# Attention and FFN on one core: another transfer rate in the planner, a mask that arrives as bf16, and the global tokens' keys in two halves

## The chip, the cores and the metric

The kernel runs on one core of a Trainium2 chip. Its time is the device time of one execution in microseconds (us). Before the change the median of three runs is 917.84 us (917.44 to 918.08). Engines are named as in the profile: PE (TensorE) multiplies matrices, DVE (VectorE), ACT (ScalarE) and POOL (GpSimd) work on vectors, SP issues the transfers (DMA). SBUF is the core's memory; PSUM is where PE leaves its results.

## The reference, cut to what matters

There are 8 batches of 8 heads, 512 local and 32 global tokens per head, and a head size of 64. A local token attends to the 32 global tokens and to the local tokens at most 32 positions away; a global token attends to all 544. The 8 x 544 rows of 512 features that result go through an FFN with 2048 hidden features. All is float32.

```python
k_all = np.concatenate([k_g, k_l], axis=2)
s_g = scale * np.matmul(q_g, k_all.transpose(0, 1, 3, 2))
out_g = np.matmul(sm(s_g), v_all)
mask = np.abs(pos[:, None] - pos[None, :]) <= 32
s_ll = np.where(mask, scale * q_l @ k_l.T, -1e9)
out_l = np.matmul(sm(concat([scale * q_l @ k_g.T, s_ll])), v_all)
...
h = x @ w_in
g = h * erf(log(1 + exp(h)))
return g @ w_out
```

## The kernel before, in words

**Attention.** The host lays the keys of a head out as 24 blocks of 32: the global block stands several times among the 16 local ones, so that any window of four neighbouring blocks is one run of 128 columns. Two heads make a pair, 32 pairs in all; a pair's queries and keys (`qk`), and its values in two parts (`va`, `vb`), come in three transfers. For a pair PE makes 2 x 16 small products, 64 rows by 32 columns of the array each (`scores`, L466). A head's 512 x 128 scores stand in one PSUM bank. Heads 0 to 27 are "early" (`PREMASK = 27`, tested on the first head of a pair): PE first multiplies the identity with a bf16 mask into the bank (two more matmuls a pair), DVE then only takes the row maximum (`TENSOR_REDUCE mx<-s`), and ACT does the exponentials. In later heads DVE adds the float32 mask and finds the maximum in one custom operation, four per head (`mask_max`, L493), and DVE or POOL subtracts. The bf16 mask and identity (`mask16`) are made by DVE at the start from the float32 constants `cs` (`shorten`, L395). Probabilities are turned for the product with the values: for the first `TURN = 26` heads by PE transposes (four a head, `tr(S..., SM..., ident)`), for the others by DVE in blocks and a trip of transfers through memory (`blocks`, `move`).

**Global tokens.** Every four heads make a tile of global tokens, 16 tiles in all (`attention_global`, L676). `whole_keys` (L685) gives each head a column group of 32 of the array: four products with 480 columns into the bank `ga`, then four with 64 into `gb`. DVE takes two maxima and combines them, ACT does two exponentials into `pg`. The first `GTURN = 7` tiles are turned by six PE transposes, the others by DVE and transfers. Then come 24 products with the values and a normalisation.

**FFN.** Weights and activations are split into a high and a low float32r part, so each product is three matmuls. Weights come in 512 KB pieces that DVE, ACT and POOL convert (`top_in`, `winh`, `winl`). FFN work of batch 0 begins while attention of the later batches runs; a second pass over the other half of the hidden features follows.

**The order.** Every piece of work is added to a `Program` with a cost per engine that may do it, a key (its priority), and the buffers it reads and writes. `schedule` (L142) plays the program with these costs on a clock of its own and writes down the order in which the engines take the work; the kernel that runs has that order fixed, and an instruction waits only for its data. A transfer costs in the plan `DMA_START`, its KB divided by `DMA_RATE` on one shared bus, `DMA_END` and `NOISE`; a piece of PE work whose inputs come from another engine or from SP counts as ready `SLACK["PE"]` later. Of the first `FEW` transfers at most `DEPTH = 5` are in flight, and the kernel enforces that with a dependency. Until `FILL` on the planner's clock, PE gets idle matmuls (`spare`) wherever the plan has nothing for it; a filler is planned at 0.11, and at 0.22 up to `COLD = 3.5`:

```python
def cools():
    return now < COLD or now < FILL and sum(h for t, h in warmth[-200:] if t > now - TICK) < HEAT
...
if e == "PE" and until[e] <= now and cools():
    fill()
```

How many fillers stand between two pieces of PE work is thus decided when the kernel is built; on the chip they run in order whether or not the data is already there. The names that follow (`HKEYS`, `QLEAD`, `VLEAD`, `STEP`, `GOFF`, `WOUT`, `SUMS` and so on) are keys and offsets of keys. `FIRST` is the number of heads that borrow FFN buffers. `GA`/`GB`, `S` and the products' banks come from six PSUM banks.

Of the kernel before, what the change touches and what calls it, by code (L numbers as in the profile page):

```python
# [30 lines left out]
QLEAD, VLEAD, RLEAD, XLEAD = (1.003, -0.044), (0.254, 0.012), -0.513, (1.017, 1.142, 1.769)  # L31
GOFF, POFF = (1.794, 2.207, 2.003), (3.921, 2.901, 4.335)
WIN, WOUT = (-1.712, -2.919, 0.936, -1.237), (9.919, 7.526, 7.174, 2.651)
LATE = (52.485, 55.408, 57.308, 59.719, 62.13, 62.366, 66.952, 69.363)
BIAS, AHEAD = 0.801, 10.994

HARM = 0.759
SLACK, PORT = {"PE": 0.827, "SP": 0.663}, 0.65
# [14 lines left out]
SWITCH, TRADE, CHOICE = 0.068, 0.092, 1  # L53

NBIAS, PREMASK = 20, 27

SPAN = 7
ORDER = ((0, 1, 2, 3, 4, 5, 6, 8, 7), (7, 0, 1, 2, 3, 4, 5, 6, 8))
SEVEN = (0, 1, 2, 3, 4, 5, 6)
SUMS = (82.024, 82.124)  # L60

TURN, GTURN = 26, 7
# [32 lines left out]
class Program:  # L95
# [3 lines left out]
    DMA_START, DMA_END, DMA_RATE = 1.62, 1.0, 300.0  # L99
# [203 lines left out]
def kernel(  # L303
# [69 lines left out]
    def fixed(t):  # L373
        b = Buf(None, None, None, None, None)
        b.ap = t
        return b

    def load(key, dst, src, kbytes, deps=(), also=()):
        add({"SP": 0.45}, key, lambda: dma(dst.ap, src), reads=deps, writes=[dst, *also], moved=kbytes)

    cs = attn.tile([P, 512 + P + 64 + 2], F32, name="cs")
    CS = fixed(cs)
    mask = cs[:, :512].rearrange("p (t k) -> p t k", k=P)
    ident = cs[:, 512 : 512 + P]
    sel = cs[:, 512 + P : 512 + P + 64]
    half = cs[:, 512 + P + 64 :]
    load(HKEYS[0][1] - QLEAD[0] + 0.001, CS, cst, 360)
    PG = fixed(attn.tile([P, NENT // 4, P], F32, name="pg"))
    M16 = Buf(mp, [P, 512], F32, "mask16", "os", 2)

# [46 lines left out]
    def attention(b, h, key):  # L437
# [76 lines left out]
        if early:  # L514
            add({"DVE": 0.6}, key, lambda: dve.tensor_reduce(MX.ap, S.ap, axis=AX.X, op=ALU.max), [S], [MX])
            add({"ACT": 1.4}, key, scaled_exps, [S, TAB], [SM, MX])
        else:
            add({"DVE": 0.85}, key, mask_max, [S, CS], [SM, MX])
# [30 lines left out]
        if h % 2 == 1:  # L549
            PT = wide([P, 4, 2 * P], f"pt_{nm}", "pt")  # L550
            move(TP, PT, 2 * P, nm, key + STEP * 2)
            for i, n in enumerate((st["kept"], nm)):
                O = psum_a([P, 4, P], f"o_{n}")
                lhs = lambda t, a, i=i: PT.ap[:, a, P * i + WB * t : P * i + WB * t + WB]
                weighted(b, h - 1 + i, n, key, O, PT, lhs, (VA, VB, XN))

    def weighted(b, h, nm, key, O, PT, lhs, tiles):
# [15 lines left out]
        add({"PE": 0.64}, key + STEP * 3, values, [PT, VA, VB], [O], heat=1040, fetch=64, mode=1)  # L573
# [102 lines left out]
    def attention_global(b, j, key):  # L676
        nm = f"{b}_{j}"
        VA = [st["va", i] for i in range(2)]
        qks = [st["qk", i] for i in range(2)]
        GA, GB = (psum_a([P, 512], f"{x}_{nm}") for x in ("ga", "gb"))  # L680
        lane, block = lambda m, hh: hh, lambda m, hh: m
        whole_keys(key, nm, qks, GA, GB)
        global_values(b, j, nm, key, GA, GB, VA, lane, block)

# [39 lines left out]
    def global_values(b, j, nm, key, GA, GB, VA, lane, block):  # L724
# [42 lines left out]
        RS = abuf([P, 1], f"gr_{nm}", "gr", 2)  # L767

        def norm():
            dve.tensor_scalar(RS.ap, O.ap[:, D : D + 1], 1e-9, None, op0=ALU.add)  # L770
            dve.reciprocal(RS.ap, RS.ap)
            dve.tensor_scalar(HALF.ap, half, RS.ap, None, op0=ALU.mult)
# [14 lines left out]
        add({"DVE": 0.5}, key + STEP * 3, norm, [O, CS], [RS, HALF])  # L787
# [72 lines left out]
    def fetch_x(ps, c, key):  # L860
# [15 lines left out]
        if 0 < c < B:  # L876
            add({"SP": 1.8}, key, by_blocks, deps, [RX], moved=1260, issues=4)
        else:
            add({"SP": 0.45}, key, whole, deps, [RX], moved=2.048 * n)
# [365 lines left out]
    for ps in range(2):  # L1245
        for c in ORDER[ps]:
# [6 lines left out]
            if ps == 1 and c in SEVEN:  # L1253
# [35 lines left out]
def _layout(q_l, k_l, v_l, q_g, k_g, v_g, moe_w_in, moe_w_out):  # L1289
# [13 lines left out]
    vw = ones(vw.transpose(0, 1, 3, 2, 4))  # L1303
    qk = np.concatenate([qT, kE], axis=3)
# [5 lines left out]
    wo = np.ascontiguousarray(moe_w_out).view(np.int64).reshape(2, 4, 2, P, 512)  # L1310
    cst = np.zeros((P, 512 + P + 64 + 2), np.float32)
# [40 lines left out]
```

## Time and profile before

| | |
|---|---|
| median of three runs | 917.84 us |
| the profiled execution | 917.4 us, of which the span of its instructions 915.6 us |
| PE, DVE, ACT, POOL busy | 98%, 69%, 58%, 35% of the span |
| mean granted PE clock | 0.998 |
| transfers | 150.49 MB, mean 164 GB/s |

Busy time is the union of an engine's instructions; PE's matmuls overlap (the next starts while one drains), so a busy PE need not be at its peak. Idle time is put down to what ended it: an engine, a transfer, or "issue" where the profile shows nothing that the engine waited for. The granted clock is 1.0 at 2.4 GHz and 0.5 at 1.2 GHz. The rows that matter stand below.

### The profile page before, as it was taken

To read this page: it belongs to the slowest core of one execution; us is meant where nothing else is said; L and a number is where in the kernel's file an instruction comes from. 1 tells how busy PE (TensorE), PEld (TensorE's weight loads), DVE (VectorE), ACT (ScalarE), POOL (GpSimd) and SP (SyncE) were. 2 spreads that over 40 slices of the span, in tenths; PEclk is the share of its full clock that TensorE was granted. 3 is DMA by queue.
4 is the path that set the end of the run, shared out by engine and by line. 5 is a ranking of instruction groups with operands and counts; after the bars stand their busy time and mean duration, and the time that the engine had idled before them with its cause. 6 is when DMAs were issued, how large, how long until landed. Compare 5 with 4: busy or idle time off the path is not lost.

```text
span 915.6 us, 23027 instructions
## 1 busy us (share of the span) xinstructions
PE 899.7 (98%) x9367; PEld 747.7 (82%) x9367; DVE 635.5 (69%) x1473; ACT 527.2 (58%) x965; POOL 322.7 (35%) x251
## 2 busy tenths in 40 slices
PE   9889999999999999999999999999999999999998
PEld 7667777776777787778888888889999999999996
DVE  2699998755556666665589897956767676767543
ACT  3476987626654566275676665557555454545561
POOL 0021446422435253251147447444343433331300
PEclk9999999999999999999999999999999999999999
DMA  8688969677987778795451510312224140402113
GB/s 330 242 310 291 327 218 306 208 232 192 340 231 239 234 225 293 223 284 188 151 161 65 190 47 0 69 47 48 66 73 102 38 138 1 138 23 94 47 46 115
DMA packets 90761, 150.49 MB, mean 164 GB/s; under 512 B 11680, under 2 KB 53664, under 8 KB 90656
## 3 DMA queue, kind: packets, MB, share of 16 engines
q1 hardware_dynamic: 90464, 148.77, 51.2%
q8 instruction: 73, 1.20, 0.5%
q10 hardware_dynamic: 192, 0.26, 0.1%
q14 instruction: 32, 0.26, 0.1%
HBM read 109.81 MB, written 39.19 MB: 163 GB/s over the span
## 4 chain that ended last, share of the span: by engine, by line
PE 79%; DVE 11%; ACT 3%; POOL 3%; issue 3%; DVEq 0%; ACTq 0%; POOLq 0%
PE op L341 34%; PE h L341 32%; PE s L341 5%; DVE top_in L362 3%; DVE top_out L362 3%; PE spare L341 2%; PE o L341 2%; PE ga L341 2%; PE go L341 1%; POOL sp L362 1%; PE s L342 1%; DVE sx L362 1%; ACT sm L343 1%; ACT gh L343 1%; POOL sx L362 1%
## 5 line engine op out<-in xcount | busy, mean ns | idle before, releaser
L341 PE MATMUL op<-wouth,gh 128*128 128x512 f32 x544 | 216.8, 398 | 0.8 <-DVE rs L362 0.6
L341 PE MATMUL op<-woutl,gh 128*128 128x512 f32 x544 | 212.4, 390 | 0.0
L341 PE MATMUL op<-wouth,gl 128*128 128x512 f32 x544 | 212.1, 390 | 0.0
L362 POOL TENSOR_TENSOR sp<-sp,hs 128x512 f32<-128x512 f32 x77 | 110.5, 1456 | 213.3 <-ACT sp L343 202.4
L341 PE MATMUL h<-xh,winh 128*128 128x512 f32 (+1 forms) x464 | 165.2, 356 | 0.0
L341 PE MATMUL h<-xh,winl 128*128 128x512 f32 (+1 forms) x464 | 162.2, 350 | 0.0
L341 PE MATMUL h<-xl,winh 128*128 128x512 f32 (+1 forms) x464 | 162.1, 349 | 0.0
L362 DVE TENSOR_TENSOR hs<-h,hs 128x256 f32<-128x256 f32 x196 | 77.3, 420 | 65.0 <-PE h L341 51.8
L341 PEld LDWEIGHTS op<-wouth,gh 128*128 128x128 f32 x544 | 102.2, 188 | 24.4 <-issue 2.0
L341 PEld LDWEIGHTS op<-wouth,gl 128*128 128x128 f32 x544 | 102.1, 188 | 22.0
L341 PEld LDWEIGHTS op<-woutl,gh 128*128 128x128 f32 x544 | 102.3, 188 | 18.5
L344 ACT ACT_TABLE_LOAD x90 | 115.5, 1283 | 2.3 <-PEq L1339 0.7
L343 ACT ACTIVATE hs<-h 128x512 f32<-128x512 f32 (+1 forms) x76 | 41.8, 553 | 119.2 <-PE h L341 118.2
L362 POOL TENSOR_TENSOR gl<-sp,gh 128x512 fp32r<-128x512 f32 x58 | 82.5, 1427 | 73.7 <-ACT gh L343 54.9
L341 PEld LDWEIGHTS h<-xh,winh 128*128 128x128 f32 x464 | 87.8, 189 | 13.3 <-issue 0.8
L343 ACT ACTIVATE gh<-sp 128x512 fp32r<-128x512 f32 x111 | 67.5, 628 | 53.8 <-PE op L341 26.4
L341 PEld LDWEIGHTS h<-xh,winl 128*128 128x128 f32 x464 | 87.8, 189 | 11.7
L343 ACT ACTIVATE sp<-hs 128x512 f32<-128x512 f32 x136 | 76.9, 623 | 35.3 <-DVE hs L362 34.9
L341 PEld LDWEIGHTS h<-xl,winh 128*128 128x128 f32 x464 | 87.9, 189 | 11.0
L362 DVE TENSOR_TENSOR gl<-sp,gh 128x512 fp32r<-128x512 f32 x78 | 74.5, 973 | 11.4 <-ACT gh L343 9.2
L343 ACT ACTIVATE sp<-sp 128x512 f32<-128x512 f32 x136 | 74.9, 620 | 0.4
L362 DVE TENSOR_TENSOR sp<-sp,hs 128x512 f32<-128x512 f32 x59 | 62.5, 1071 | 9.9 <-ACT sp L343 9.3
(181 smaller groups left out, 1525.6 us busy)
## 6 DMA issues: line engine op xcount, KB each, us to landing
vb<-in_vB_dram SPq DMA_DIRECT2D x32, 650.0 KB, 6.0
qk<-in_qk_dram SPq DMA_DIRECT2D x30, 656.0 KB, 7.0
rx<-xsc SPq DMA_DIRECT2D x52, 256.0 KB, 5.2
va<-in_vA_dram SPq DMA_DIRECT2D x32, 390.0 KB, 5.9
px<-tp SPq DMA_DIRECT2D x76, 128.0 KB, 5.3
pt<-px SPq DMA_DIRECT2D x19, 512.0 KB, 5.3
raw_in<-in_w_in_dram SPq DMA_DIRECT2D x16, 512.0 KB, 4.4
xsc<-xT SPq DMA_DIRECT2D x32, 256.0 KB, 5.0
```

The source lines that it names most:

```text
L341: pe = lambda n, *a, **k: pinned(nc.tensor.matmul(n, *a, **k))
L342: tr = lambda *a, **k: pinned(nc.tensor.transpose(*a, **k))
L343: act = lambda *a, **k: pinned(nc.scalar.activation(*a, **k))
L344: table = lambda name: pinned(nc.scalar.preload_act_table_set(name))
L362: return lambda *a, **k: pinned(f(*a, **k))
```

## The change

- The planner's transfer: `DMA_RATE` 300 to 400 KB/us, start 1.62 to 1.5, end 1.0 to 0.9, `NOISE` 1.096 to 0.4. The cost of an activation fetch in blocks is given as 1700 KB in place of 1260.
- The constants come in three transfers in place of one. The first 160 KB are the mask and the identity as bf16, made by the host, into `mask16`; then identity, selector and halves as float32 (100 KB planned) into `ci`; later, by the key `MLEAD`, the float32 mask (262 KB planned) into `cs`. In the plan's keys the first stands just ahead of the first `qk`, the second just behind it. `shorten` on DVE is gone.
- From global tile 6 on (`GSPLIT = 6`, ten of 16 tiles) `half_keys` replaces `whole_keys`: eight products of 384 columns, one for each of the four column groups and two row groups of the array: the keys are cut into two halves that stand in different column groups, the even and odd head of a pair go to `ga` and `gb`. DVE takes two maxima, exchanges them between the halves in four small operations and combines them in a fifth; ACT does four exponentials. The global block that is then met twice has its values zeroed by the host (`vw[..., NWIN - 1] = 0.0`).
- `PREMASK` 27 to 26 (13 pairs with the mask from PE, where there were 14), `TURN` 26 to 24, `GTURN` 7 to 8, `FIRST` 12 to 16, `FEW` 68 to 70, `FILL` 52.16 to 53.627.
- The normalisation of a global tile keeps its sum in PSUM and multiplies with a tensor operation in place of a scalar one.
- `NBIAS` 20 to 19, and keys, offsets and weights of the planner are set anew (`HKEYS`, `STEP`, `GKEY`, `VLEAD`, `XLEAD`, `GOFF`, `WIN`, `WOUT`, `LATE`, `SUMS`, `HARM`, `SLACK["SP"]`, `SWITCH`, `TRADE`). `MERGE` and `PLAIN` are new and off.

```diff
-SINCE, COLD, FILL, TICK, HEAT = 0.75, 3.5, 52.16, 3.41, 3200
-HKEYS = ((0, -7.978), (4, -4.315), (22, 1.593), (28, 6.473), (64, 43.98))
-STEP, GKEY = 0.008, (-0.119, -0.115, -0.139)
+SINCE, COLD, FILL, TICK, HEAT = 0.75, 3.5, 53.627, 3.41, 3200
+HKEYS = ((0, -7.978), (4, -4.315), (22, 1.593), (26, 7.644), (64, 44.103))
+STEP, GKEY = 0.023, (-0.152, -0.148, -0.172)
...
-FIRST = 12
+FIRST = 16
-DEPTH, FEW = 5, 68
-LANES, NOISE = 8, 1.096
+DEPTH, FEW = 5, 70
+LANES, NOISE = 8, 0.4
-NBIAS, PREMASK = 20, 27
+NBIAS, PREMASK = 19, 26
+MLEAD = -5.966
-SUMS = (82.024, 82.124)
-TURN, GTURN = 26, 7
+SUMS = (81.085, 83.737)
+TURN, GTURN = 24, 8
+GSPLIT = 6
...
-    DMA_START, DMA_END, DMA_RATE = 1.62, 1.0, 300.0
+    DMA_START, DMA_END, DMA_RATE = 1.5, 0.9, 400.0
...
-    load(HKEYS[0][1] - QLEAD[0] + 0.001, CS, cst, 360)
+    load(HKEYS[0][1] - QLEAD[0] - 0.001, M16, cst[:, :320], 160, short=320)
+    load(HKEYS[0][1] - QLEAD[0] + 0.001, CS, cst[:, 832:], 100)
+    load(MLEAD, CM, cst[:, 320:832], 262)
-    def shorten():
-        m, i = halves()
-        dve.tensor_scalar(m, cs[:, :512], -1.0, -(2.0**33), op0=ALU.is_lt, op1=ALU.mult)
-        dve.tensor_copy(i, ident)
-    if PREMASK:
-        add({"DVE": 0.6}, HKEYS[0][1], shorten, [CS], [M16])
...
+        if 2 * b + j < GSPLIT:
+            lane, block = lambda m, hh: hh, lambda m, hh: m
+            whole_keys(key, nm, qks, GA, GB)
+        else:
+            lane, block = lambda m, hh: hh // 2 * 2 + m // 3, lambda m, hh: hh % 2 * 3 + m % 3
+            half_keys(key, nm, qks, GA, GB)
+    def half_keys(key, nm, qks, GA, GB):
+        def scores():
+            for i in range(2):
+                for f in range(2):
+                    for r, T in enumerate((GA, GB)):
+                        c0 = WB * (2 * i + f)
+                        _, q, k = qks[i]
+                        pe(T.ap[c0 : c0 + WB, :384], q()[D * r : D * r + D, :SG],
+                           k()[D * r : D * r + D, 384 * f : 384 * f + 384], start=True, stop=True)
+        add({"PE": 0.85}, key, scores, [*qks[0][0], *qks[1][0]], [GA, GB], heat=768, fetch=32, mode=1)
+        def both():
+            M = GA.ap[:, 400:402]
+            for r, T in enumerate((GA, GB)):
+                dve.tensor_reduce(M[:, r : r + 1], T.ap[:, :384], axis=AX.X, op=ALU.max)
+            for c in range(4):
+                o = WB * (c ^ 1)
+                dve.tensor_scalar(NM.ap[WB * c : WB * c + WB, 2:4], M[o : o + WB, :], -scale, None, op0=ALU.mult)
+            dve.scalar_tensor_tensor(NM.ap[:, 0:2], M, -scale, NM.ap[:, 2:4], op0=ALU.mult, op1=ALU.min)
+        add({"DVE": 1.5}, key, both, [GB], [GA, NM])
+        def exps():
+            for r, T in enumerate((GA, GB)):
+                src = T.ap[:, :384].rearrange("p (m x) -> p m x", x=P)
+                dst = PG.ap[:, 3 * r : 3 * r + 3, :]
+                for x in (slice(0, WB), slice(2 * WB, 4 * WB)):
+                    act(dst[:, :, x], src[:, :, x], AF.Exp, bias=NM.ap[:, r : r + 1], scale=scale)
...
+    c16[:, :512] = np.where(cst[:, :512] < 0, 0xD000, 0)
+    c16[:, 512:] = np.where(cst[:, 512 : 512 + P] > 0, 0x3F80, 0)
+    cst = np.concatenate([c16.view(np.float32), cst], axis=1)
```

## Rows read from the trace of the kernel before

**Rows 1.** The head of the page: the span, and the busy time of each engine with its share and its instructions.

```profile
span 915.6 us, 23027 instructions
PE 899.7 (98%) x9367; PEld 747.7 (82%) x9367; DVE 635.5 (69%) x1473; ACT 527.2 (58%) x965; POOL 322.7 (35%) x251
```

**Rows 2.** The waits of PE, summed over the span: what waited, for what, us in total, times, longest. Two rows carry most of it.

```profile
PE s L341 <- issue: 4.2, 3, 2.2
PE ga L341 <- issue: 2.5, 1, 2.5
```

**Rows 3.** Busy time of each engine in stretches of the span: the stretch and its length in us, then PE, PEld, DVE, ACT, POOL with their instructions, the granted PE clock, the share of the transfer engines, GB/s.

```profile
0.00:10.00 10.00, 9.23 (x58) 7.17 (x59) 0.56 (x2) 1.28 (x1) 0.94 (x5) 1.00 0.81 311
...
30.00:40.00 10.00, 10.00 (x206) 6.95 (x196) 6.33 (x17) 4.12 (x16) 0.00 (x0) 0.83 0.57 187
...
140.00:150.00 10.00, 10.00 (x140) 7.53 (x123) 9.79 (x32) 8.93 (x16) 5.95 (x5) 1.00 1.05 281
200.00:300.00 100.00, 97.30 (x1307) 75.22 (x1305) 60.88 (x199) 56.86 (x95) 38.66 (x29) 1.00 0.82 248
31.00:34.20 3.20, 3.20 (x14) 1.69 (x12) 1.97 (x5) 0.00 (x0) 0.00 (x0) 0.52 0.85 275
```

**Rows 4.** PE's timeline at the start: when a group of equal instructions began, how long it ran, which tile it wrote and read, rows*columns of the array, shape, count.

```profile
0.77 9.61 PE L341 MATMUL spare<-const-bfloat16-1.0 128*128 128x256 bf16 x59 [0.77 <-PEq L1339]
10.22 0.59 PE L341 MATMUL s<-mask 128*128 128x512 bf16 x2
10.74 1.16 PE L341 MATMUL s<-qk 64*32 64x128 f32 x64
11.83 3.53 PE L341 MATMUL spare<-const-bfloat16-1.0 128*128 128x256 bf16 x30
15.20 0.59 PE L341 MATMUL s<-mask 128*128 128x512 bf16 x2
...
17.84 1.01 PE L341 MATMUL ga<-qk 64*32 64x480 f32 x8
18.66 0.29 PE L341 MATMUL gb<-qk 64*32 64x64 f32 x8
18.89 0.73 PE L341 MATMUL spare<-const-bfloat16-1.0 128*128 128x256 bf16 x5
...
20.72 0.60 PE L342 MATMUL s<-cs,sm 128*128 128x128 f32 x4
21.16 1.06 PE L341 MATMUL spare<-const-bfloat16-1.0 128*128 128x256 bf16 x8
```

**Rows 5.** The first and the second transfer of queries and keys: when SP issued them (timeline of SP's queue), and their KB and us from issue to landing (transfers of these stretches).

```profile
0.74 0.40 SPq L348 DMA_DIRECT2D qk<-in_qk_dram  x1
2.60 0.48 SPq L348 DMA_DIRECT2D qk<-in_qk_dram  x1
...
qk<-in_qk_dram SPq DMA_DIRECT2D x1, 656.0 KB, 4.0
qk<-in_qk_dram SPq DMA_DIRECT2D x1, 656.0 KB, 7.2
```

**Rows 6.** DVE's timeline at the start: the two operations that make the bf16 mask.

```profile
5.68 0.43 DVE L362 TENSOR_SCALAR mask<-cs 128x512 bf16<-128x512 f32 x1 [5.68 <-DMA cs<-in_cst_dram]
6.03 0.22 DVE L362 CAST mask<-cs 128x128 bf16<-128x128 f32 x1
```

**Rows 7.** Transfers in two stretches: the columns of rows 3.

```profile
5.00:10.00 5.00, 5.00 (x39) 4.13 (x38) 0.56 (x2) 0.00 (x0) 0.00 (x0) 1.00 1.02 419
60.00:120.00 60.00, 56.93 (x1153) 43.23 (x1152) 57.31 (x137) 48.43 (x134) 15.15 (x12) 1.00 0.93 323
```

**Rows 8.** Operations on a global tile's scores on DVE and ACT, count, then least, median and greatest ns, first and last start.

```profile
L362 DVE TENSOR_REDUCE gm<-ga x16: 610/648/659, 18.9 to 404.5; 128x1 f32<-128x480 f32 x16
L362 DVE TENSOR_REDUCE gm<-gb x16: 185/214/219, 19.5 to 406.4; 128x1 f32<-128x64 f32 x16
L362 DVE TENSOR_SCALAR gn<-gm x16: 172/212/216, 19.7 to 408.0; 128x1 f32<-128x1 f32 x16
L343 ACT ACTIVATE pg<-ga,gn x16: 639/662/680, 21.0 to 410.1; 128x480 f32<-128x480 f32 x16
L343 ACT ACTIVATE pg<-gb,gn x16: 303/316/342, 21.5 to 410.6; 128x64 f32<-128x64 f32 x16
```

**Rows 9.** PE's timeline where a global tile is turned: from the first transpose into `ga` to the first instruction after those into `gb`.

```profile
41.23 0.49 PE L342 MATMUL ga<-cs,pg 128*128 128x128 f32 x3
41.56 0.49 PE L342 MATMUL gb<-cs,pg 128*128 128x128 f32 x3
41.89 0.94 PE L341 MATMUL spare<-const-bfloat16-1.0 128*128 128x256 bf16 x7
```

**Rows 10.** Groups of DVE's instructions by shape: busy us, mean ns of one, idle time before them and what ended it.

```profile
L362 DVE CUSTOM_DVE_ANT_0 sm<-s,cs 128x128 f32<-128x128 f32 x144 | 31.7, 282 | 8.9 <-PE s L341 5.8 <-POOL xl L362 3.1
L362 DVE STREAM_TRANSPOSE tp<-sm 128x512 f32<-128x512 f32 x38 | 25.8, 693 | 8.4 <-DMA px<-tp 8.3
L362 DVE TENSOR_REDUCE mx<-s 128x4 f32<-128x512 f32 x28 | 18.3, 681 | 12.6 <-PE s L341 12.6
```

**Rows 11.** PE's timeline at two of its longest gaps, which end in the middle of a block of small matmuls.

```profile
29.50 0.88 PE L341 MATMUL ga<-va,gt 128*32 128x65 f32 x44 [2.45 <-issue]
62.97 0.91 PE L341 MATMUL s<-qk 64*32 64x128 f32 x45 [2.19 <-issue]
```

More of the change, by code (lines that the diff above doesn't have):

```diff
@@ L376, in fixed, with load @@
         return b
[L378 to L386, printed above, removed]
-    load(HKEYS[0][1] - QLEAD[0] + 0.001, CS, cst, 360)
-    PG = fixed(attn.tile([P, NENT // 4, P], F32, name="pg"))
+    def load(key, dst, src, kbytes, deps=(), also=(), short=None):
+        add({"SP": 0.45}, key, lambda: dma(dst.ap[:, :short] if short else dst.ap, src), reads=deps, writes=[dst, *also], moved=kbytes)
+    cs, ci = attn.tile([P, 512], F32, name="cs"), attn.tile([P, P + 64 + 2], F32, name="ci")
+    CM, CS = fixed(cs), fixed(ci)
+    mask = cs.rearrange("p (t k) -> p t k", k=P)
+    ident = ci[:, :P]
+    sel = ci[:, P : P + 64]
+    half = ci[:, P + 64 :]
     M16 = Buf(mp, [P, 512], F32, "mask16", "os", 2)
+    load(HKEYS[0][1] - QLEAD[0] - 0.001, M16, cst[:, :320], 160, short=320)
+    load(HKEYS[0][1] - QLEAD[0] + 0.001, CS, cst[:, 832:], 100)
+    load(MLEAD, CM, cst[:, 320:832], 262)
     def halves():
@@ L393, in halves @@
         return t[:, :512], t[:, 512 : 512 + P]
-    def shorten():
-        m, i = halves()
-        dve.tensor_scalar(m, cs[:, :512], -1.0, -(2.0**33), op0=ALU.is_lt, op1=ALU.mult)
-        dve.tensor_copy(i, ident)
-    if PREMASK:
-        add({"DVE": 0.6}, HKEYS[0][1], shorten, [CS], [M16])
+    PG = fixed(attn.tile([P, NENT // 4, P], F32, name="pg"))
     add({"POOL": 0.7}, -99, lambda: pool.memset(PG.ap, 0.0), writes=[PG])
@@ L517, in attention @@
         else:
-            add({"DVE": 0.85}, key, mask_max, [S, CS], [SM, MX])
+            add({"DVE": 0.85}, key, mask_max, [S, CM], [SM, MX])
         if early:
@@ L551, in attention @@
             move(TP, PT, 2 * P, nm, key + STEP * 2)
+            both = []
             for i, n in enumerate((st["kept"], nm)):
@@ L554, in attention, with weighted @@
                 lhs = lambda t, a, i=i: PT.ap[:, a, P * i + WB * t : P * i + WB * t + WB]
-                weighted(b, h - 1 + i, n, key, O, PT, lhs, (VA, VB, XN))
-    def weighted(b, h, nm, key, O, PT, lhs, tiles):
+                weighted(b, h - 1 + i, n, key, O, PT, lhs, (VA, VB, XN), both if MERGE else None)
+    def weighted(b, h, nm, key, O, PT, lhs, tiles, both=None):
         VA, VB, XN = tiles
@@ new lines, in attention_global @@
+        global_values(b, j, nm, key, GA, GB, VA, lane, block)
+    def half_keys(key, nm, qks, GA, GB):
[5 more added lines that the diff above has]
+                        _, q, k = qks[i]
+                        pe(
+                            T.ap[c0 : c0 + WB, :384],
+                            q()[D * r : D * r + D, :SG],
+                            k()[D * r : D * r + D, 384 * f : 384 * f + 384],
+                            start=True,
+                            stop=True,
+                        )
+        add({"PE": 0.85}, key, scores, [*qks[0][0], *qks[1][0]], [GA, GB], heat=768, fetch=32, mode=1)
+        NM = abuf([P, 4], f"gn_{nm}", "gn", 2)
+        def both():
[13 more added lines that the diff above has]
+                    act(dst[:, :, x], src[:, :, x], AF.Exp, bias=NM.ap[:, r : r + 1], scale=scale)
+        if not cleared:
+            cleared.append(add({"POOL": 0.7}, key, lambda: pool.memset(PG.ap, 0.0), writes=[PG]))
+        add({"ACT": 1.1}, key, exps, [GA, GB, NM, TAB], [PG])
@@ L1252 @@
                     sums(u, SUMS[u])
-            if ps == 1 and c in SEVEN:
+            if ps == 1 and c in SEVEN[PLAIN:]:
                 X = seven_x(c, s - XLEAD[2])
```

46 lines of the change are left out of this document (30 added, 16 removed).

## The prediction

> **What bounds the kernel now.** I read the head of the page first. PE is busy for 899.7 of 915.6 us, DVE for 635.5 [rows 1]. PE's own waits say the same: nothing on another engine holds it for more than a microsecond in sum, and the two rows that carry anything are 4.2 and 2.5 us of "issue" [rows 2]. So the end moves when PE gets less to do, or when PE does something useless less often. The stretches show where the second is possible [rows 3]: from 200 to 300 us PE is busy for 97.30 of 100 us with real work, DVE for 60.88; in the first 10 us PE is busy too, but DVE has 0.56 us of work and ACT 1.28, and in 30 to 40 us both have still half their time free. PE's timeline tells what it does there [rows 4]: 59 fillers from 0.77 to 10.22 us, 30 more from 11.83 to 15.20. Fillers stand in a fixed order, so the first scores start at 10.22 us however early their data is in. From about 140 us DVE is full as well (9.79 of 10 us [rows 3]), PE too. Hence two places matter: the first 60 us, which fillers and latency set, and the rest, which PE's work sets.
>
> The sum is made against the profiled execution: 917.4 us, 915.6 us of span and 1.8 us around it. The median of the runs, 917.84, lies 0.44 above it, which I add at the end.
>
> **The keys in halves (ten tiles).** `whole_keys` takes PE from 17.84 to 18.89 us, 1.05 us [rows 4]. In it eight instructions of 480 columns (each of the four products is two) take 18.66 - 17.84 = 0.82 us in four column groups: 960 columns in each group one after the other, 0.85 ns a column. The 64 score instructions of 128 columns take 11.83 - 10.74 = 1.09 us. Were only four at work at once, that would be 2048 columns one after the other and 0.53 ns each, faster than the same type runs in `ga`; with eight at once it is 1024 at 1.06 ns. So the row groups do run side by side, and scores are laid out as `half_keys` is (even and odd heads in two row groups and two banks). Sixteen instructions of 384 columns in eight lanes are 768 columns in each: 0.66 us at 0.85 ns, 0.82 at 1.06. I take 0.73, the middle: 10 x (1.05 - 0.73) = **-3.2 us** (-2.3 to -3.9), all on the engine that sets the end.
>
> **Less and more for PE.** One pair fewer gets its mask from PE: 10.74 - 10.22 = 0.52 us [rows 4], **-0.5**. Two heads fewer are turned by PE: 21.16 - 20.72 = 0.44 us each [rows 4], **-0.9**. One global tile more is: 41.89 - 41.23 = 0.66 us [rows 9], **+0.7**.
>
> **The start.** How many fillers are written follows from the planner's constants; their price is in the trace. Before, the plan has `qk` (671 KB) and `cs` (360 KB) on the bus: 1.62 + 1031/300 + 1.0 + 1.096 = 7.15, then 0.6 for `shorten`, 0.13 of latency and 0.827 of slack: 8.71. From 0.75 to 3.5 that is 12 fillers at 0.22, to 8.71 another 47 at 0.11: the 59 of the row [rows 4]. On the chip the mask was ready at 6.25 us [rows 6] and `qk` at 0.74 + 4.0 = 4.74 [rows 5], so 4 us were given away. After, `mask16` and `qk` stand first: 1.5 + 831/400 + 0.9 + 0.4 + 0.827 = 5.70, which is 12 + 20 = 32 or 33 fillers. The 26 that go cost 3.37/30 = 0.112 us each (those from 11.83 to 15.20 [rows 4]): 2.9 us, and the scores start at about 7.3 us. `qk` is then issued 0.45 us later, behind 160 KB that take 0.4 us at 419 GB/s [rows 7], and lands by 5.6: early enough. `shorten`'s 0.65 us of DVE [rows 6] lay in idle time and bring nothing by themselves. By the same count the second pair's operands are ready in the plan at 10.30 (2668 KB), and its mask starts at about 11.8 us in place of 15.20; its data lands at 2.60 + 7.2 = 9.8 us [rows 5].
>
> Does this reach the end? DVE and ACT have room behind it until 40 us [rows 3], and the next loads wait for buffers that those scores free. Against it, the constants grow from 353 to 522 KB, 0.4 us of a full bus at 419 GB/s [rows 7], of which half may show. I take 2.9 - 0.2 = **-2.7 us**; the ends are 0 (the following pairs are held by something else) and -3.4.
>
> **DVE and ACT.** A half tile has two maxima over 384 columns (0.648 x 384/480 = 0.52 us each [rows 8]) and five small operations at the 0.21 us of `gn` [rows 8], 2.1 us against 0.65 + 0.21 + 0.21 = 1.07: +1.0 a tile. ACT has 2 x (0.34 + 0.42) = 1.5 us (interpolated between 64 and 480 columns [rows 8]) against 0.98. Eight of the ten tiles lie beyond 180 us, where DVE and ACT have 40% free [rows 3]; that hides them, and without that cover they would cost PE up to 1.0 us each. Two lie in the stage in which DVE is full. There two heads more are also turned by DVE (0.693 us each) and two more have the mask added there (4 x 0.282 against 0.681, +0.4 each [rows 10]). That makes 2.0 + 1.4 + 0.9 = 4.3 us of DVE at the one place where it is full. POOL has 4 us in 10 free of work there and more [rows 3], and PE has FFN matmuls to put in front. I take **+0.8** between 0 and 4.3, near the free end because POOL can share.
>
> The normalisation in PSUM, the buffers of `FIRST`, the float32 mask (wanted only from head 26 on, long after it lands) and the keys of the second pass move no work on or off PE: 0, with +-2 us for what a new order does to two things that PE's waits show, the "issue" gaps of 2.45 and 2.19 us [rows 11] and the stretch from 31.00 to 34.20 us in which the granted clock is 0.52 [rows 3], the level of 1.2 GHz, right behind the first of these gaps; it costs half of 3.2 us.
>
> **Sum:** -3.2 - 0.5 - 0.9 + 0.7 - 2.7 + 0.8 = -5.8; 917.4 - 5.8 = 911.6, and with 0.44 **912.0 us**.
>
> A page speaks against the planner's new rate. The first 10 us show 419 GB/s [rows 7], but between 60 and 120 us the transfer engines are 93% busy and move 323. The Trainium skill, "DMA: Bandwidth & Descriptors", section "Where 436 GB/s comes from", says that between HBM and SBUF the HBM side binds at some 358 GB/s a core. If that held at the start, the second pair's 2668 KB would be 0.8 us later than planned and the start's term -1.9 in place of -2.7; the 419 of the trace, with one core at work, does not bear it out.
>
> **The rivals.**
> *The start is absorbed.* Later pairs are spaced by chains on ACT and DVE and by the bus, and at 50 to 60 us the same point is reached as before. For it: the bus is 100% busy in 5 to 10 us [rows 7]. Against it: nothing is full in 30 to 40 us [rows 3]. Without the -2.7: 914.7 us.
> *The whole head is packed better.* Between 15 and 60 us there are more fillers, the two gaps and the low clock; a plan with truer loads can take some 4 us more out of them: 908.0.
> *Loads come late (slower).* At 400 KB/us the plan expects the bytes of 60 to 120 us, 323 x 60 = 19.4 MB, in 48.4 us; they took 60 [rows 7]. If the order leans on that, PE stands before loads that aren't there, with no fillers in the order. All of it is 11.6 us: 917.4 - 5.8 + 11.6 + 0.4 = 923.6; it decides from 7.7 us on. For it: the bus is nearly full there. Against it: DVE is busy for 57.31 of these 60 us [rows 7], so that loads are not the only thing that PE's work there waits for; and no load stands in PE's waits [rows 2], though under a plan that expected less than the chip gave.
> *Only four lanes at once.* Then a half tile takes 16 x 384/4 = 1536 columns, 1.31 us at 0.85 ns, and ten cost +2.6 in place of -3.2: 917.8, no change. The score rows speak against it.
>
> **How the numbers follow.** A difference of 0.2% (1.8 us) is about what a measurement of this kernel can tell from no change. The likeliest case has 0.42, with a range of its own from 909.5 to 914.3. Absorbed start 0.23, better packed head 0.13, late loads 0.11, four lanes 0.04, and 0.07 for small losses of order that eat the gain (near 917). Faster: 0.42 + 0.23 + 0.13 less some 0.03 of their edges, 0.75; slower 0.11 and 0.02 of other mishaps, 0.13; the same 0.12. The range runs from 906.5 (the packed head and a little more) to 918.5, which takes in the four lanes and leaves out late loads.
>
> **What the changed profile would show.** The first `s<-mask` at about 7.3 us behind 32 or 33 fillers, the second at about 11.8. In tiles 6 to 15 sixteen instructions of 64x384 in 0.66 to 0.82 us from the first to the next work. 26 `s<-mask` in place of 28 (13 pairs), 96 in place of 104 `s<-cs,sm` (24 heads). The first FFN matmul near 61 us; before it follows the scores that end the second gap, at some 63.9 us [rows 11]. It would be wrong if PE's waits name a transfer or DVE for more than 3 us, if the first FFN matmul comes no earlier, or if a half tile takes over 1 us.

## The result, and the profile after

The changed kernel takes 926.09 us (median of 13 runs, 921.22 to 930.05); the kernel before took 917.76 in the same job (13 runs, 914.82 to 921.73). The ratio is 1.0087 (95% interval [1.0066, 1.0108]): slower, by 0.9%. Here and below a ratio holds a kernel against the kernel before in the same job; it is worked out from all runs and need not be the quotient of the two medians. The forecast was 912.0 with a range of 906.5 to 918.5, so both the sign and the range were wrong. The profiled execution took 928.16 us, 926.3 of it span.

The head of the page after and its chain of waits, to be held against [rows 1]:

```profile
span 926.3 us, 22999 instructions
PE 900.2 (97%) x9340; PEld 747.2 (81%) x9340; DVE 636.1 (69%) x1569; ACT 535.9 (58%) x985; POOL 247.0 (27%) x198
...
PE 64%; DMA 11%; DVE 3%; SPq 2%; issue 1%; ACT 0%; DVEq 0%; ACTq 0%
PE op L344 32%; PE h L344 30%; DMA px<-tp 6%; DMA xsc<-xT 3%; SPq L351 2%; DVE tp L365 1%; DMA rx<-xsc 1%; PE o L344 1%; DMA gt<-px 1%; PE s L344 1%; PE go L344 1%; DMA qk<-in_qk_dram 1%; DVE sm L365 0%; PE ga L344 0%; DVE xT L365 0%
```

PE is as busy as before (900.2 us against 899.7) although it has less to do. POOL is busy 75.7 us less (322.7 to 247.0 us). And 11% of the chain, some 100 us, now runs over transfers, `px<-tp` above all; the chain of the kernel before has none:

```profile
PE 79%; DVE 11%; ACT 3%; POOL 3%; issue 3%; DVEq 0%; ACTq 0%; POOLq 0%
```

The start came about as forecast. PE's timeline after, for [rows 4]:

```profile
0.77 6.04 PE L344 MATMUL spare<-const-bfloat16-1.0 128*128 128x256 bf16 x32 [0.77 <-PEq L1405]
6.65 0.59 PE L344 MATMUL s<-mask 128*128 128x512 bf16 x2
...
8.26 2.97 PE L344 MATMUL spare<-const-bfloat16-1.0 128*128 128x256 bf16 x25
11.07 0.59 PE L344 MATMUL s<-mask 128*128 128x512 bf16 x2
...
49.98 0.48 PE L344 MATMUL h<-xh,winh 128*128 128x512 f32 x1
```

The first scores start 3.6 us earlier than before, the second pair 4.1, the first FFN matmul at 49.98 in place of 63.8. None of it reaches the end. Where it goes shows in a landmark that both kernels have, the first matmul of the second pass (its instructions in both kernels: least, median and greatest ns, then first and last start in us):

```profile
L341 PE MATMUL h<-xh,s1h x56: 278/283/384, 582.5 to 857.6; 128*128 128x256 f32 x56
```

```profile
L344 PE MATMUL h<-xh,s1h x56: 283/283/283, 594.8 to 867.8; 128*128 128x256 f32 x56
```

After is 12.3 us late there; from there to the end it needs 926.3 - 594.8 = 331.5 us against 915.6 - 582.5 = 333.1. So the loss lies wholly ahead of the second pass. Up to there the busy times (columns of rows 3) are these, first before, then after:

```profile
0.00:582.50 582.50, 572.00 (x7333) 451.64 (x7333) 424.88 (x1041) 352.55 (x690) 214.03 (x159) 1.00 0.67 217
```

```profile
0.00:594.80 594.80, 573.34 (x7307) 451.50 (x7308) 421.09 (x1110) 367.97 (x721) 172.64 (x135) 0.99 0.66 214
```

PE stands 10.5 us before and 21.5 after, 11.0 us longer. Its busy time grows by 1.3 us. Busy times from 100 to 450 us (columns of rows 3), before:

```profile
100.00:450.00 350.00, 346.55 (x4761) 269.72 (x4748) 237.32 (x717) 211.17 (x380) 135.86 (x101) 1.00 0.77 242
```

and after, with four stretches inside it:

```profile
100.00:450.00 350.00, 335.11 (x4749) 258.61 (x4749) 230.23 (x767) 201.65 (x376) 106.34 (x82) 0.98 0.77 242
...
108.00:111.40 3.40, 3.40 (x84) 2.62 (x69) 3.37 (x5) 3.37 (x6) 2.32 (x2) 0.51 0.02 5
145.60:149.00 3.40, 3.40 (x41) 3.03 (x42) 0.76 (x3) 0.98 (x2) 0.00 (x0) 0.50 1.06 242
217.20:220.60 3.40, 3.40 (x51) 2.72 (x41) 2.08 (x6) 2.57 (x4) 2.52 (x2) 0.51 0.45 143
306.00:309.40 3.40, 3.40 (x10) 2.64 (x9) 2.80 (x19) 0.93 (x4) 1.92 (x2) 0.50 0.89 256
```

From 100 to 450 us the bytes and the share of the transfer engines are the same (242 GB/s, 0.77), but PE stands 346.55 - 335.11 = 11.4 us longer, and four times runs at 1.2 GHz, 3.4 us each, which by an estimate (half of each stretch) costs 4 x 1.7 = 6.8 us more. Both kernels have one such stretch ahead of 60 us. So up to the second pass 11.0 us more of idle time and 6.8 of the clock stand against some 5.5 us less of work, which makes the 12.3. What PE stands for: its waits and, below them, two rows of ACT's and one of DVE's, all from 60 to 460 us.

```profile
PE s L344 <- DVE xn L365: 3.5, 1, 3.5
PE o L344 <- DMA pt<-px: 3.0, 2, 2.8
PE go L344 <- DMA gt<-px: 2.7, 2, 1.9
PE o L344 <- issue: 2.6, 2, 2.2
PE ga L344 <- issue: 1.9, 1, 1.9
...
ACT os L346 <- DMA part<-os: 11.8, 7, 3.0
...
ACT xh L346 <- DMA rx<-xsc: 10.7, 5, 3.7
...
DVE tp L365 <- DMA px<-tp: 19.0, 10, 5.1
```

In [rows 2] PE waits for no transfer at all. In this stretch of the kernel before ACT stands 2.1 us for `rx<-xsc` and 0.6 for `part<-os`, and for no other transfer; in the changed kernel all its waits for transfers sum to 25.8 us. DVE's wait for `px<-tp` has doubled:

```profile
DVE tp L362 <- DMA px<-tp: 9.4, 5, 3.6
```

`px<-tp`, `pt<-px` and `gt<-px` are the trips through memory that turn probabilities; `xsc` and `rx` bring attention's results to the FFN. The longest gap names DVE, and DVE's own timeline shows two things behind it. First PE, then DVE, then POOL, in the changed kernel:

```profile
102.36 1.16 PE L344 MATMUL s<-qk 64*32 64x128 f32 x64
107.01 0.61 PE L344 MATMUL s<-mask 128*128 128x512 bf16 x2 [3.50 <-DVE xn L365]
```

```profile
101.95 0.76 DVE L365 CAST xh<-rx 128x512 fp32r<-128x512 f32 x2 [1.59 <-DMA rx<-xsc]
...
102.70 3.37 DVE L365 TENSOR_TENSOR xl<-rx,xh 128x512 fp32r<-128x512 f32 x2
...
106.54 0.42 DVE L365 TENSOR_TENSOR xn<-s,rs 128x256 f32<-128x256 f32 x1
```

```profile
102.46 3.06 POOL L365 TENSOR_TENSOR xl<-rx,xh 128x512 fp32r<-128x512 f32 x2 [10.11 <-DVE xh L365]
```

DVE stands 1.59 us for `rx`, then converts it, and `xn`, which frees the bank that PE wants, is queued behind. The wait explains at most 1.59 of the 3.50 us: the two `xl` on DVE take 1.69 us each beside POOL's two, while operations of this shape (`xl<-xT,xh`) took 0.69 us earlier in the same kernel. A wait that names an engine has to be followed one step back.

### The profile page after: what moved, and what is told of

It is laid out like the page before. It is cut to its first block, busy times and chain, and to the rows that moved or that the text cites. A ratio compares the mean times of both kernels' runs of the same rounds, so it can differ in the third digit from the quotient of the medians.

```text
span 926.3 us, 22999 instructions
## 1 busy us (share of the span) xinstructions
PE 900.2 (97%) x9340; PEld 747.2 (81%) x9340; DVE 636.1 (69%) x1569; ACT 535.9 (58%) x985; POOL 247.0 (27%) x198
## 4 chain that ended last, share of the span: by engine, by line
PE 64%; DMA 11%; DVE 3%; SPq 2%; issue 1%; ACT 0%; DVEq 0%; ACTq 0%
PE op L344 32%; PE h L344 30%; DMA px<-tp 6%; DMA xsc<-xT 3%; SPq L351 2%; DVE tp L365 1%; DMA rx<-xsc 1%; PE o L344 1%; DMA gt<-px 1%; PE s L344 1%; PE go L344 1%; DMA qk<-in_qk_dram 1%; DVE sm L365 0%; PE ga L344 0%; DVE xT L365 0%
## 5 line engine op out<-in xcount | busy, mean ns | idle before, releaser
L365 POOL TENSOR_TENSOR sp<-sp,hs 128x512 f32<-128x512 f32 x73 | 99.6, 1381 | 268.2 <-ACT sp L346 267.9
L346 ACT ACTIVATE gh<-sp 128x512 fp32r<-128x512 f32 x94 | 56.8, 628 | 55.7 <-POOL sp L365 33.5
L365 DVE TENSOR_TENSOR gl<-sp,gh 128x512 fp32r<-128x512 f32 x97 | 75.3, 792 | 17.8 <-ACT gh L346 16.2
L365 POOL TENSOR_TENSOR gl<-sp,gh 128x512 fp32r<-128x512 f32 x39 | 54.0, 1390 | 42.7 <-ACT gh L346 36.1
L365 DVE TENSOR_TENSOR sp<-sp,hs 128x512 f32<-128x512 f32 x63 | 55.0, 883 | 10.1 <-ACT sp L346 9.9
```

The lines of the kernel that those rows point to most:

```text
L346: act = lambda *a, **k: pinned(nc.scalar.activation(*a, **k))
L365: return lambda *a, **k: pinned(f(*a, **k))
```

## The experiments

The main theory (A): the plan at 400 KB/us believes that the trips through memory are back earlier than they are, and the order puts their users too early. For one trip, `pt<-px`, rows bear out its first half, as an estimate: on an empty bus the new model plans 1.5 + 524/400 + 0.9 + 0.4 = 4.1 us and the old one 1.62 + 524/300 + 1.0 + 1.096 = 5.5; from issue to landing (median) it took, in the changed kernel and in the one before:

```profile
pt<-px SPq DMA_DIRECT2D x20, 512.0 KB, 5.8
```

```profile
pt<-px SPq DMA_DIRECT2D x19, 512.0 KB, 5.3
```

Its rivals: the added DVE and ACT work of the half tiles; the earlier start, which only moves a jam; and that this schedule was found by tuning, so that any new order loses. The first kernels undo one part of the change, or make one part alone in the kernel before.

**The transfer model, both ways.** In the changed kernel, back to the old model, with all keys as changed:

```diff
-    DMA_START, DMA_END, DMA_RATE = 1.5, 0.9, 400.0
+    DMA_START, DMA_END, DMA_RATE = 1.62, 1.0, 300.0
-LANES, NOISE = 8, 0.4
+LANES, NOISE = 8, 1.096
```

(and the activations' fetch back to 1260 KB.)

> The changed kernel with the planner's old transfer model (start 1.62, end 1.0, 300 KB/us, NOISE 1.096, a blocked fetch counted as 1260 KB); all else as changed. Theory A (the plan counts on transfers that land later than planned, so PE meets its values before they are there, between 100 and 440 us): the stalls on pt<-px and gt<-px go and most of the 8.3 us comes back, under 919 us, the first scores near 9.5 us again. Theory B (the new keys and the longer chain of the half tiles make the stalls): still 923 us or more.

Measured: 928.91 us, ratio 1.0135 [1.0097, 1.0172]. PE waits for no transfer any more, ACT for 2.7 us in 60 to 460 us in place of 25.8, yet no time comes back. DVE's waits for transfers hardly fall (23.4 us against 26.8; 12.3 in the kernel before). Its PE waits of that stretch:

```profile
PE o L344 <- ACT pg L346: 2.9, 1, 2.9
PE s L344 <- issue: 2.1, 2, 1.7
PE go L344 <- DVE xT L365: 2.0, 1, 2.0
```

The loss moved to ACT and DVE and towards the end of attention (the 1.2 GHz stretches are at 424, 434 and 591 us). The keys were set for the other model; this run alone can't clear or convict the rate. The reverse, the new model alone in the kernel before (the diff above turned around):

> The kernel before with the new transfer model alone (1.5, 0.9, 400 KB/us, NOISE 0.4, blocked fetch 1700 KB). Theory A: slower than before by 4 us or more, although its first scores start near 7 us, with PE waiting for px and pt transfers and the clock at half for some stretches between 100 and 440 us. Theory B: as fast as before or up to 3 us faster.

Measured: 938.62, ratio 1.0237 [1.0192, 1.0282], 20 us slower, with 27.0 us of ACT's waits for transfers, as in the changed kernel (25.8), and 41.4 us of DVE's (60 to 460 us). Two rows of ACT's, and PE's largest:

```profile
ACT xh L343 <- DMA rx<-xsc: 16.4, 4, 6.2
...
ACT os L343 <- DMA part<-os: 10.1, 5, 3.2
...
PE o L341 <- issue: 10.7, 6, 3.0
```

PE itself stands for a transfer for only 0.4 us in this kernel, against what theory A expected; 15.1 us of its waits are "issue", whose cause no run shows. And a replan with unchanged keys could cost that much by itself. So a third kernel uses the new model only for the first 14 transfers, whose order is thus planned anew as well:

```diff
+ first, end, rate, noise = (1.5, 0.9, 400.0, 0.4) if len(lanes) < 14 else (1.62, 1.0, 300.0, 1.096)
```

> The kernel before, planned with the new transfer model for the first 14 transfers and the old one for all others. If the rate of 400 KB/us in the later stages is what makes the stalls of the new plans (theory A): waits of ACT for transfers between 60 and 460 us back under 5 us (27 with the new model throughout), and the time back from 938 to 920 us or less. If an earlier start shifts everything into worse places: 925 us or more, ACT's waits for transfers still over 15 us.

Measured: 926.65, ratio 1.0105 [1.0067, 1.0143]. Between the two kernels lie 938.62 - 926.65 = 12.0 us (the two jobs' medians of the kernel before differ by 1.2), and with them go ACT's waits for transfers (27 us to 0.5), most of DVE's (41.4 to 14.4) and half of PE's "issue" (15.1 to 6.8). That the model of the later transfers makes the 12 us is likely, but these are two different orders as well. The other 9 are not back, which theory A had expected; in that new order PE stands for `xn`, `xg` and "issue" between 20 and 150 us.

The same two-part model with the changed kernel's keys:

> The changed kernel planned with the new transfer model for the first 14 transfers and the old one for all others (blocked fetch 1260 KB). Theory A: no waits of PE for transfers, ACT's under 5 us, and faster than the changed kernel by 3 us or more if the keys allow it. If the keys were fitted to the new model: 926 us or more, with the loss at the end of attention, 400 to 460 us, as with the old model throughout.

Measured: 934.0, ratio 1.0152 [1.0119, 1.0185]. No PE wait for a transfer, 5.1 us on ACT, but 4.6 and 3.2 us of "issue" between 350 and 450 us, and a loss near 600. As in the first run, the transfer model of before gives nothing with the changed keys. DVE still waits 22.8 us for transfers.

**Half tiles.** Whole keys in all tiles of the changed kernel:

```diff
-GSPLIT = 6
+GSPLIT = 16
```

> The changed kernel with the whole keys in all 16 global tiles. Theory A: 2 to 3 us slower than the changed kernel (ten tiles at 1.05 in place of 0.81 us), the same stalls. Theory B: the stalls shrink because DVE and ACT have 1.0 and 0.5 us less in ten tiles, 920 us or less.

Measured: 929.35, ratio 1.0138 [1.0097, 1.0179]: 3.3 us above the changed kernel by the medians of two jobs, with the same long gap (4.0 us for `xn`). The halves are not the cause. The halves alone in the kernel before, first replanned with their costs:

> The kernel before with the keys in halves from global tile 6 on and nothing else of the change. Theory A: faster than before by some 2.4 us (ten tiles at 0.81 in place of 1.05 us). Theory B: slower than before, with new waits of PE for pg or gt.

Measured: 923.7, ratio 1.0072 [1.0046, 1.0098], slower, where theory A expected a gain; the waits of PE for `pg` or `gt` that the other theory expected are not there either. Here too the order is new. Then with the order of before kept exactly (planned as whole keys, executed as halves from tile 6 on), the two maxima in SBUF:

```diff
-        whole_keys(key, nm, qks, GA, GB)
+        whole_keys(key, nm, qks, GA, GB, 2 * b + j >= GSPLIT)
...
+    dve.tensor_scalar(NM.ap[WB * c : WB * c + WB, 2:4], M.ap[o : o + WB, :], -scale, None, op0=ALU.mult)
```

> The kernel before, planned with the whole keys' operations and costs in every tile, so that the order of all engines is the one of before; at run time tiles 6 to 15 do the half keys' matmuls, maxima and exponentials. If the new order is what costs (theory A, now in the form: any newly made order loses to the one that was fitted on the chip), this is faster than before by 2 to 2.5 us, 915.5 us, where the newly planned half keys were 5 us slower. If the half tile's longer chain on DVE and ACT is what costs (theory B), it is slower than before by 3 us or more.

Measured: 923.96, ratio 1.0075 [1.0049, 1.0102]. This looked like a verdict against the halves until its timeline was read. POOL, then DVE, in that kernel:

```profile
152.42 5.44 POOL L363 TENSOR_TENSOR xl<-rx,xh 128x512 fp32r<-128x512 f32 x4
```

```profile
153.04 4.84 DVE L363 TENSOR_SCALAR gn<-gm 32x2 f32<-32x2 f32 x4
157.92 0.16 DVE L363 SCALAR_TENSOR_TENSOR gn<-gm,gn 128x2 f32<-128x2 f32 x1
```

Four operations on 64 numbers each took 1.2 us apiece beside POOL's (the median of this shape in SBUF is 0.16). PE's gap behind them is 3.48 us, and 3.4 us at 1.2 GHz follow it: 5.2 us, about the whole loss. The change has these maxima in PSUM, so this loss belongs to the experiment. The halves only from tile 8 on (`GSPLIT = 8`), where DVE has more room:

> As the last half-key run (order of before kept), but with the half keys from global tile 8 on, so that tiles 6 and 7, which lie in the stage where DVE is full, keep the whole keys. If DVE in that stage is what the half tiles cost (the +0.8 of the prediction, too small): the gap near 159 us goes, and the kernel is 1.5 to 2 us faster than before (eight tiles at 0.24 us), 916 us. If the chain of a half tile costs wherever it stands: 921 us or more, with waits of PE for pg left.

Measured: 917.7, ratio 1.0006 [0.9985, 1.0028], still with the maxima in SBUF. Then in PSUM, as in the change, again from tile 6 on:

```diff
+        MM = lambda: GA.ap[:, 400:402] if halves else M.ap
```

> As the half keys in the order of before from tile 6 on, but the two maxima of a half tile stand in PSUM (as the changed kernel has them) and not in SBUF, where four operations of 32x2 took 4.84 us beside POOL in tile 7. If that sharing with POOL was the loss: no gap near 159 us, each small operation 0.16 us at most 0.2, and 1.5 to 2.5 us faster than before, 915.5 us. If DVE's full stage or the chain is the loss: 920 us or more, the gap still there.

Measured: 916.43 against 919.0, ratio 0.9974 [0.9949, 1.0]. The small operations now take 0.166 us at most (those of all ten tiles, in this kernel):

```profile
L363 DVE TENSOR_SCALAR gn<-ga x40: 149/155/166, 132.3 to 408.9; 32x2 f32<-32x2 f32 x40
```

So the halves are worth some 2.5 us where the order stays as it was (0 to 4.7 by the interval). Ten times what PE's timeline of the changed kernel gives for one tile (below) is close to that.

**The start.** The order of before, with 27 and 5 fewer fillers in the first two blocks:

```diff
+        if op.fn is prog.idle[1]:
+            run += 1
+            if block < 2 and run > keep[block]:
+                continue
```

> The kernel before in its own order, with 27 of the first 59 fillers and 5 of the next 30 left out, so that as many are left as in the changed kernel. If the start's gain reaches the end: faster than before by 2 to 3.4 us. If something else holds the later pairs (the first rival of the prediction): within 1 us of before, first FFN matmul still at 63 to 64 us.

Measured: 916.89 against 918.42, ratio 0.999 [0.9968, 1.0013]. The first FFN matmul comes at 58.6 in place of 63.8 us, and then the lead goes. The stretch from 50 to 60 us in this kernel, and PE's wait from 0 to 100:

```profile
50.00:60.00 10.00, 6.99 (x221) 5.30 (x210) 9.76 (x24) 6.27 (x20) 2.62 (x2) 0.94 0.98 358
...
PE s L341 <- issue: 4.0, 2, 2.5
```

DVE is full in it (9.76 of 10 us), as it was in the kernel before (9.83), and now the transfer engines too (0.98 against 0.76). PE stands for 3 us, which the profile puts down to "issue"; which of the two takes the lead away isn't shown. Fewer fillers together with halves from tile 8 on:

> The order of before with the half keys from tile 8 on and with 27 and 5 of the first fillers left out. If the two gains add: 3 to 4 us faster than before, 914.5 us, faster than both kernels. If the start's gain is absorbed: 916 us.

Measured: 917.47, ratio 1.0003 [0.9981, 1.0025]; nothing is left of the start here either.

**Does any new order lose?** A small step of one key in the kernel before, and one in the changed kernel:

```diff
-STEP, GKEY = 0.008, (-0.119, -0.115, -0.139)
+STEP, GKEY = 0.010, (-0.119, -0.115, -0.139)
```

> The kernel before with STEP 0.010 in place of 0.008, which changes no work and no cost, only the order that the planner writes. Theory A in its new form: slower than before by 4 us or more, with other stalls and clock drops. Theory C (what the changed plans believe of the chip, rate or costs, makes the loss): within 2 us of before.

```diff
-HKEYS = ((0, -7.978), (4, -4.315), (22, 1.593), (26, 7.644), (64, 44.103))
+HKEYS = ((0, -7.978), (4, -4.315), (22, 1.593), (26, 7.644), (64, 44.123))
```

> The changed kernel with the key of the last head 0.02 later, no other work or cost: another order again. Theory A in its new form: 920 to 935 us, the stalls at other places than 103, 142, 214 and 302 us. Theory C: within 2 us of the changed kernel, the stalls at the same places.

Measured: before with the step 915.47, ratio 0.9968 [0.9943, 0.9994], a little faster; the changed kernel with its step 935.94 in a single run, again with PE before `pt` and `gt` (10.5 us for transfers, ACT 26.6). "Any new order loses" falls with the first, but not "most new orders lose": of the eight kernels here that were planned anew from one of the two, seven have a longer time than the one that they start from (two of them by less than the noise tells). That can be a part of the 20, 9 and 5 us above. From the second, a single run, I only take that the stalls stay on the same transfers.

**The loads made light.** The sharpest test leaves both orders as they are and takes bytes off the bus. From head 16 on, only the keys of `qk`, a quarter of `va` and a quarter of `vb` are loaded, and the products read what is there; the values of those heads are not the reference's.

```diff
-                load(key - QLEAD[b > 1], QKB, qk[b, p], 671)
+                q0 = SQ if b * H + h >= 16 else 0
+                part_load(key - QLEAD[b > 1], QKB, qk[b, p], 671, slice(q0, QK))
...
+            la, lb = (3, 5) if b * H + h >= 16 else (12, 20)
```

> The changed kernel in its own order, but from head 16 on each pair loads only its keys, a quarter of va and a quarter of vb (1.06 MB of 1.70 MB a pair less; the products read what is there, so the numbers of those heads are not the reference's; no instruction of PE, DVE or ACT is left out). If late transfers make the stalls of the new order (theory A): PE's waits for pt and gt and ACT's waits for transfers between 60 and 460 us (25.8 us) go to under 6 us, and the time falls by 6 us or more, below 920 us. If the order loses on DVE and PE's own gaps: within 2 us of the changed kernel.

> The same smaller loads in the kernel before, in its own order. Theory A: within 2 us of before, which waits for no transfer on PE and 2.7 us on ACT. If lighter loads help any order by freeing ports or the instruction fetch: 5 us or more faster than before.

Measured: changed kernel 911.33, ratio 0.9892 [0.9856, 0.9928]; kernel before 913.75, ratio 0.9948 [0.992, 0.9976]. The trips get faster by it: the median of `pt<-px` falls from 5.8 to 4.2 us in the changed kernel. Light loads are worth 926.09 - 911.33 = 14.8 us to the changed order (two jobs; 17.9 by the difference of the ratios) and 917.18 - 913.75 = 3.4 us to the old one (4.8 by its ratio). So 11 to 13 us of the gain belong to the changed order alone, more than the 8.3 that it loses. The 3.4 us lie between what the two cases expected; PE's "issue" falls by 2.8 us there (4.2 to 1.4, 60 to 460 us). The stretch of before once more, first the changed kernel with light loads (and its waits for transfers, from 60 to 460 us), then the old one:

```profile
100.00:450.00 350.00, 345.26 (x4825) 268.33 (x4824) 246.94 (x790) 216.25 (x398) 111.19 (x85) 1.00 0.63 183
...
PE o L344 <- DMA pt<-px: 0.6, 1, 0.6
PE go L344 <- DMA gt<-px: 0.5, 1, 0.5
...
ACT os L346 <- DMA part<-os: 5.5, 4, 2.3
...
ACT xh L346 <- DMA rx<-xsc: 4.7, 3, 2.6
```

```profile
100.00:450.00 350.00, 348.98 (x4786) 272.17 (x4774) 238.06 (x719) 212.84 (x383) 136.08 (x102) 1.00 0.62 178
```

PE has 10.2 of its 11.4 us back, its waits for transfers fall from 5.7 to 1.1 us, and the mean granted clock from 100 to 450 us is 1.00 again, with one stretch at 1.2 GHz left of four. ACT's waits for transfers fall from 25.8 to 13.5 us, not below 6 as expected, and DVE's from 26.8 to 9.2. What stays is the gap before `xn`, PE first, then DVE:

```profile
106.47 0.60 PE L344 MATMUL s<-mask 128*128 128x512 bf16 x2 [1.85 <-DVE xn L365]
```

```profile
102.14 3.38 DVE L365 TENSOR_TENSOR xl<-rx,xh 128x512 fp32r<-128x512 f32 x2
```

DVE waits for no transfer here, and PE still stands 1.85 of the 3.50 us, behind the two slow `xl` beside POOL's. That part of the loss is not a late transfer. The division of work between POOL and DVE as a whole is not what costs: it is the same in this fast kernel (POOL 246.7 us, DVE 637.2). The second pass starts at 578.6 us, 16.2 earlier than in the changed kernel. With light loads the changed order is the faster of the two by 2.4 us of the medians, though the intervals of the two ratios overlap.

**Is there a version that beats both?** The step of the key with fewer fillers, and the step with halves in PSUM:

> The kernel before with STEP 0.010 and with at most 32 and 25 fillers left in the first two blocks, the two edits to the kernel before that did not lose. If the start's gain adds to it: 913 to 914 us, faster than both kernels by more than 0.3%. If it is absorbed as in the order of before: 915.5 us, as with STEP alone.

> The same in the order that STEP 0.010 gives, which was 0.3% faster than before. If the half tiles' gain adds: 912 to 914 us, faster than both kernels. If the order gives it back: 915 to 916 us.

Measured: 917.68, ratio 1.0003 [0.9975, 1.0031]; and 915.34 against 919.0, ratio 0.9974 [0.9945, 1.0002]. With fewer fillers the gain of the step isn't to be seen either. The step alone (0.9968), the halves in PSUM (0.9974) and both together (0.9974) are the best of what ran with all its loads. They can't be told apart; only the step's interval lies below 1 throughout.

## Why the prediction was wrong

- **Which step failed.** The one that said that the rest of the change (buffers, keys of the second pass) would "move no work on or off PE: 0, with +-2 us" for what a new order does. The planner's new rate had a term only at the start. That no work moves onto PE fits the profile (busy for 900.2 us against 899.7, with some 6.8 us of the new slow stretches in it), but when its inputs come was priced at nothing. In its place the runs show 11.0 us more of idle time on PE ahead of the second pass, and 11 to 13 us that light loads give back to the changed order beyond what they give to the old one. That the order waits for transfers is shown by this; that the planner's new rate is what made it so is not (below). The rival that has this mechanism, "loads come late (slower)", was on record at 923.6 us, 2.5 below the median, with a chance of 0.11 and outside the range.
- **Why the rival was rated low, and what was wrong in that.** It was placed in 60 to 120 us, where the bus is 93% busy [rows 7], and its price came from there. The stalls lie from 103 to 336 us, one of them in that stretch, and the mean share from 100 to 450 us is 0.77. What is late is not the loads of `qk`, for which PE stands nowhere in 60 to 460 us, but the chains through memory (`px<-tp`, `pt<-px`, `gt<-px`, `rx<-xsc`, `part<-os`), with an engine at either end. I looked for loads in PE's waits [rows 2] and found none, under a plan that expected less than the chip gave, as the text said itself; and I took DVE's 57.31 busy us as a reason against it. It is not one: a 1.59 us wait of DVE for `rx` there reaches PE, as a part of 3.50 us. The sentence that no other engine holds PE for more than a microsecond in sum is true row by row only: DVE's six rows sum to 3.5 us. And looking at PE's rows alone hid that DVE already waited 9.4 us for `px<-tp` in the kernel before.
- **The clock** was costed once, at the old gap of 31 us. Four of the new gaps, of 1.93 to 3.50 us, were followed by 3.4 us at 1.2 GHz each, by the estimate 1.7 us more each time. Two of the four end on transfers, one on `xn`, one on "issue".
- **Half tiles, -3.2.** Right in mechanism, smaller in size. PE's timeline of the changed kernel at tile 6:

```profile
132.11 0.53 PE L344 MATMUL ga<-qk 64*32 64x384 f32 x3
...
132.94 0.50 PE L344 MATMUL h<-xh,winh 128*128 128x512 f32 x1
```

  0.83 us to the next work where I took 0.73; another tile gave 0.81. With 1.05 for a whole tile that is ten times 0.22 to 0.24, -2.2 to -2.4, at the near end of the bounds (-2.3). "Only four lanes" (1.31 us) falls.
- **Mask and turning, -0.5, -0.9, +0.7.** The counts are as forecast (26 and 96 instructions); no run tried them alone.
- **Start, -2.7.** Every landmark came as early as forecast or earlier (6.65 us against 7.3, 11.07 against 11.8, 49.98 against "near 61"), and the value was 0, the term's upper end: "the start is absorbed" was right for this term. Two runs on the order of before and one on the order of the step show it; the place is behind 50 us, where DVE and the transfer engines are full. I had looked for room only up to 40 us, where DVE had 3.7 of 10 us free and not half.
- **DVE and ACT, +0.8.** The halves on the order of before gained about what PE's shorter tiles give, so the cover held there, as far as an interval of 0 to 4.7 us tells. In the changed order it wasn't measured by itself.
- **What was to show it wrong** did: PE's waits name DVE for 3.5 us in one row (5.2 in all rows from 60 to 460 us) and transfers for 5.7.
- **What stays open.** Whether the planner's rate or the keys make the changed order wait. The old rate and the two-part rate in the changed kernel removed PE's and most of ACT's waits for transfers, not DVE's, and not the time. No set of keys made for the old model was tried together with the rest of the change. `FIRST`, the constants in three transfers and the planner's weights were not tried alone, and no run takes the two slow `xl` apart.

## What to carry to other kernels

Don't judge a planner's transfer cost by the bus at the start: look up how long each round trip through memory takes from issue to landing in the stage where its user stands, and hold the plan against that. The order is fixed, and each user that it puts too early holds what is queued behind it, on every engine and not only on the one that sets the end. Measure each part of a change on the old order before adding the next. To ask whether an order waits for transfers, keep the order and take bytes off the bus. Before counting a gain at the start, look for the first stretch behind it in which an engine or the bus is full; here three such gains were gone after one.

## What the runs showed of the hardware

- Four gaps of PE (3.50, 2.77, 1.93 and 2.21 us) were each followed by a stretch of 3.4 us at a granted clock of 0.50 or 0.51, and so cost their length and, by an estimate, 1.7 us more. The length of the gap alone doesn't tell: the one of 1.90 us that ends at 82.16 us wasn't followed by one (1.00 from 80 to 88.5 us), nor was one of 2.19 us in the kernel before (1.00 from 62.97 to 70), but one of 1.85 us in the changed kernel with light loads was (0.54 from 107.5 to 110.9).
- Four DVE operations on 32x2 numbers in SBUF took 4.84 us beside four POOL operations on the activations (1.2 us each), and 0.155 us each (median) with the operand in PSUM. The Trainium skill, "SBUF — State Buffer", section "Who interferes with whom", says that DVE and GpSimd share a pair of ports, which one of them holds for a whole instruction. The rows agree: POOL's own operations there took 5.44 / 4 = 1.36 us, and the DVE ones came through at about that pace, however small.
- Two DVE operations of 128x512 numbers (`xl`) took 3.37 us beside two of POOL's in the changed kernel, and 0.69 us each earlier in it.
- PE's gaps put down to "issue" (2.2 and 1.9 us after, 2.5 before) end at or inside blocks of small matmuls in nearly every kernel here. They move with the order, and light loads shrink their sum in the order of before from 4.2 to 1.4 us (60 to 460 us); no run was made to find their cause.
- One program differs by 0.8% from run to run (914.82 to 921.73 us in 13 runs of the kernel before), so a part worth 2 us is hardly told from nothing even with 12 runs.
